# One DMA order for the loads and the weights, wider engine choice and a state without its zero blocks, in an RWKV-5 attention and squared-ReLU MLP kernel

## The chip, the cores and the metric

The kernel runs on one core of a Trainium2 chip. The metric is the device time of one launch in microseconds. The core has five engines that each work through their own queue in order: TensorE (PE in the profile, with its weight loads shown apart as PEld), VectorE (DVE), ScalarE (ACT), GpSimd (POOL) and SyncE (SP), which here only issues DMAs. Sixteen DMA engines move the data. An instruction that waits holds back everything behind it on its queue.

## What is computed

The reference is a linear-attention recurrence with decay, followed by a two-layer MLP without biases. With batch B=4, H=8 heads, S=768 steps and head width D=48:

```python
for t in range(S):
    cur = einsum('bhd,bhe->bhde', u[None] * kt, vt)
    y[:, :, t] = einsum('bhd,bhde->bhe', rt, state + cur)
    state = w[None, :, :, None] * state + einsum('bhd,bhe->bhde', kt, vt)
x = y.transpose(0, 2, 1, 3).reshape(B * S, H * D)     # 3072 x 384
h = x @ w_in                                          # 384 x 2048
r = np.maximum(h, 0.0)
return (r * r) @ w_out                                # 2048 x 384
```

Inputs and output are float32. The kernel multiplies in bfloat16 and accumulates in float32.

## The kernel before

**Units.** The sequence is cut into 6 chunks of C=128 steps. A unit is one chunk of one batch, so there are NU=24, numbered chunk by chunk over the four batches: unit n continues the state that unit n-4 left. Heads go in pairs, with each head padded from 48 to 64 rows, so a pair fills the 128 partitions.

**Attention of one unit** (lines 435 to 560). Three loads bring kt, rt and vt (192 KB each). `kw` and `rw` multiply k and r by powers of the decay and write them side by side into the buffer krp in bfloat16. ScalarE casts v to `vb`. `rk`, `rku`, `du` and `dv` make the term of the current step: r times k, times u, summed over a head, times v. krp is transposed to `rkT`: for units 0 to 9 (`NT = 10`) by TensorE and a copy, from unit 10 on by a DMA transpose that SyncE issues (line 481). `am` multiplies k with r inside the chunk, `mask` keeps the strict triangle (`AT`), `ym` multiplies AT with v and adds r times the state, and `yb` adds dv. The result is transposed to `xt`, again by TensorE or by DMA (line 573).

**State.** `kvm` makes the new product of k and v for each pair in one matmul. As two heads share a matmul, its output has a 2 by 2 grid of blocks: the two diagonal ones are the heads' own, the other two mix heads. `sma` adds the product to the old state, `smo` multiplies by the decay over the chunk `wc`, and `sbo` casts the result to bfloat16 for `ym` of unit n+4. The tiles `sm`, `sb` and `wc` are 128 x (4 pairs, 2 heads, 48), that is 384 columns, and `wc` is zero in the mixed blocks.

**MLP.** Two units make a pair (L=2, 256 rows). For each of 8 parts of the hidden layer, `m1` runs 6 matmuls (line 591), `relu` goes to VectorE or ScalarE, `sq` to ScalarE or GpSimd, and `m2` runs 2 matmuls for each unit (line 620). `osb` copies a finished unit out of PSUM and SyncE stores it.

**Weights.** w_in and w_out come in five pieces each (`PIECES`, of 1, 1, 2, 2 and 2 of the 8 parts), issued by GpSimd, which alone casts on the way.

**The order.** All of this is declared as operations with a cost per engine, a key (a due time), dependences and buffers. The function `schedule` places them one after another in a model of the engines and of the DMA, always the one that can start first; on a tie the lower key wins, with a surcharge (`away`, 8.0) for an engine that is not the operation's first. The instructions are then emitted in that order, so the order on every queue is fixed by the plan, while on the chip each waits for what it really needs. `port=True` marks products that use the port shared by VectorE and GpSimd. The plan keeps such a product on VectorE from starting before the last instruction of GpSimd ends, and GpSimd from starting inside one of VectorE. The helper `both` (line 440) gives a product GpSimd as its first engine, and VectorE as the second one for units below `NDVE`.

**The feed.** The loads of units 0 to 3 come first. Then the ten weight pieces, w_in and w_out by turns: the first two wait for the last load of unit 2, and each later one for the piece three before it. The first load of unit 4 waits for the eighth of the ten pieces. These gates are real waits; the other entries in the list of dependences of a load (the load four before it, and the last one) only guide the plan. Each of kt, rt and vt has 8 buffers (`NLOAD`).

```python
for n in range(4):
    for nm in ("kt", "rt", "vt"):
        load(n, nm)
w_ops = []
for i in range(len(PIECES) - 1):
    for which in ("in", "out"):
        w_ops.append(weights(i, which, w_ops[-3] if len(w_ops) >= 3 else units[2]["vt"]))
for n in range(4, NU):
    for nm in ("kt", "rt", "vt"):
        load(n, nm, w_ops[-3] if n == 4 and nm == "kt" else None)
```

**In the profile** most products have line 324 and most copies line 329 (ScalarE) or 331 (VectorE), the lines of the helpers, so they are told apart by their tiles: `krp<-kt,wk` is kw, `krp<-rt,wr` is rw, `sm<-bank,sm` is sma, `sm<-sm,wc` is smo, `sb<-sm` is sbo. L390 is the loads, L411 and L413 the weights, L516 am, L535 and L540 ym, L634 the stores, L310 and L313 memsets at the start.

Of the kernel before, what the change touches and what calls it, by code (L numbers as in the profile page):

```python
# [8 lines left out]
F32 = mybir.dt.float32  # L9
BF16 = mybir.dt.bfloat16  # L10
AF = mybir.ActivationFunctionType
ALU = mybir.AluOpType
# [24 lines left out]

def schedule(ops, depth, limits, free, away, warm_until=0.0, noise=None, keyf=None, bias=0.0):

    rings = {r: [] for r in depth}  # L40
# [11 lines left out]
    lastP = lastV = None  # L52
    base = {}

# [50 lines left out]
    while ready:  # L105
        best = None
        for o in ready:
            t = base.get(o)
            if t is None:
                t = 0.0  # L110
                for d, lat in o.deps:
                    t = max(t, d.end + (d.lat if lat is None else lat))
                base[o] = t
            if best is not None and t + bias * o.key > best[0][0]:
# [5 lines left out]
            if best is not None and t + bias * o.key > best[0][0]:  # L120
                continue
            chosen = ()
            if any(bf.ring in limits for bf in o.takes):
                got = pick_banks(o, t)
                if got is None:
                    continue
                t, chosen = got
            first = True
            for e in o.eng:
                s = max(t, free[e])  # L130
                if e == "V" and o.port and lastP is not None and lastP[1] > s:
                    s = lastP[1]
                elif e == "P" and lastV is not None and lastV[2] and lastV[1] > s >= lastV[0]:
                    s = lastV[1]
                rank = (s + bias * o.key, o.key + (0.0 if first else away.get(e, 0.0)), s)
# [6 lines left out]
        cost = o.eng[e]  # L142
        if noise is not None:
            cost *= noise(o)
# [36 lines left out]
def kernel(  # L181
# [11 lines left out]
    nc = tc.nc  # L193
# [19 lines left out]
    NT = 10  # L213
    NDVE = 6
    PIECES = (0, 1, 2, 4, 6, 8)
    AHEAD = 4
    LAG = 4.0
    DEPTH = 4

# [80 lines left out]
    wr = const.tile([128, H, D], F32)  # L300
    wc = const.tile([128, NP, 2, D], F32)
    ub = const.tile([128, H, D], F32)
# [6 lines left out]
    for i in range(NPADS):  # L309
        nc.vector.memset(make["krp"][i], 0.0)  # L310
    make_identity(nc, identb)
    make_upper_triangular(nc, smask, val=1.0, diag=False)
    nc.vector.memset(wc, 0.0)  # L313

# [48 lines left out]
    def emit_wcb(e):  # L363
        for i in range(2):
            rows = slice(i * PAD, i * PAD + D)
            nc.scalar.copy(wc[rows, :, i, :], wcs[rows, :, None].to_broadcast([D, NP, D]))

    o_wc = op("wc", {"A": 0.6}, 1.1, [o_wcs], emit_wcb)
    o_ub = op("ub", {"V": 0.5, "A": 0.45}, 0.5, [o_ubp],
# [14 lines left out]
    def load(n, nm, gate=None):  # L384
# [20 lines left out]
    def weights(i, which, gate):  # L405
# [3 lines left out]
        def f(e):  # L409
# [12 lines left out]

    for n in range(4):
        for nm in ("kt", "rt", "vt"):
            load(n, nm)
    w_ops = []
    for i in range(len(PIECES) - 1):
        for which in ("in", "out"):
            w_ops.append(weights(i, which, w_ops[-3] if len(w_ops) >= 3 else units[2]["vt"]))
    for n in range(4, NU):  # L430
        for nm in ("kt", "rt", "vt"):
            load(n, nm, w_ops[-3] if n == 4 and nm == "kt" else None)


    for n in range(NU):
# [42 lines left out]
        else:  # L478
# [3 lines left out]
                    out=T("rkT").rearrange("p w a c -> p (w a) c"), in_=T("krp").rearrange("p w h d -> p (w h d)")),  # L482
                takes=[X["rkT"]], uses=[X["krp"]], lat=0.05, dma=(0.7, 1.05, 0.95))
        if c < NCH - 1:
# [13 lines left out]
            old = units[n - B]["sm"] if c else None  # L498
            SM = lambda x: make[x.ring][x.slot]
            if c:  # L500
                q["sma"] = op(f"sma{n}", {"V": 0.48}, K + 3, [q["kvm"], units[n - B]["smo"]],
                              tt(lambda sm=sm: SM(sm), kvp, lambda old=old: SM(old), ALU.add), uses=[sm, kv_p, old])
                q["smo"] = op(f"smo{n}", both(0.96, 0.48), K + 5, [q["sma"]],
                              tt(lambda sm=sm: SM(sm), lambda sm=sm: SM(sm), lambda: wc, ALU.mult), uses=[sm], port=True)
            else:
                q["smo"] = op(f"smo{n}", {"V": 0.48}, K + 5, [q["kvm"], o_wc],
                              tt(lambda sm=sm: SM(sm), kvp, lambda: wc, ALU.mult), uses=[sm, kv_p])
# [55 lines left out]
    for j in range(NU // L):  # L563
# [111 lines left out]
```

## Time and profile before

| | |
|---|---|
| Time, median of 3 runs | 190.45 us (190.41 to 193.27) |
| The profiled execution | 192.72 us |
| Its span, from first to last instruction | 191.0 us |
| Mean granted TensorE clock | 0.991 |
| HBM read, written | 20.65 MB, 4.72 MB |

The profile is of a single execution. A group line reads: source line, engine, operation, output and inputs with their shapes, count; then busy time in us and mean ns of one; then the idle time of that engine just before, with what ended it. A line of the waits reads: who waited, for what, total us, how often, the longest. A line of the timeline reads: start, duration, engine, line, operation, with the idle time before it in brackets. In the table by stretch, the granted clock, the share of the DMA engines and the GB/s stand at the end of a line.

### The profile page before, as it was taken

How to read it: one execution, taken by the hardware profiler on the slowest of the kernel's cores; microseconds unless marked ns; L12 is line 12 of the kernel's file. 1: busy time of each engine (PE TensorE's matmuls, PEld its weight loads, DVE VectorE, ACT ScalarE, POOL GpSimd, SP SyncE). 2: the span in 40 equal slices, each digit the busy share in tenths (PEclk: the TensorE clock that was granted, in tenths of full speed). 3: DMA queues.
4: the chain of work that ended last, by engine and by line, in shares of the span. 5: the costliest groups of instructions: out<-in, count | busy, mean ns of one | idle time of the engine just before them, and what ended most of it. 6: DMA issues, size and time to landing. Idle time of an engine off the chain costs nothing.

```text
span 191.0 us, 4343 instructions
## 1 busy us (share of the span) xinstructions
PE 172.1 (90%) x1653; PEld 121.7 (64%) x1653; DVE 125.7 (66%) x217; ACT 109.3 (57%) x195; POOL 139.4 (73%) x158
## 2 busy tenths in 40 slices
PE   6998679798979999949998896999999999999992
PEld 2654356575757767637766675777777677777760
DVE  6265366487776668735687577689688786765741
ACT  3663347257669596624857547467665464663641
POOL 2899988499899989993888899799999994000000
PEclk9999999999999999997999999999999999999999
DMA  5999899989899999993989999435632444040202
GB/s 108 204 207 146 118 181 162 204 170 244 170 207 245 189 199 192 217 220 89 201 174 151 257 183 121 128 75 152 87 79 85 80 131 101 0 106 21 88 0 84
DMA packets 103256, 27.56 MB, mean 144 GB/s; under 512 B 96065, under 2 KB 103234, under 8 KB 103234
## 3 DMA queue, kind: packets, MB, share of 16 engines
q1 hardware_dynamic: 99088, 24.13, 61.4%
q0 software_dynamic: 4128, 3.15, 11.8%
q8 instruction: 13, 0.21, 0.5%
q14 instruction: 9, 0.07, 0.2%
q10 hardware_dynamic: 18, 0.00, 0.0%
HBM read 20.65 MB, written 4.72 MB: 133 GB/s over the span
## 4 chain that ended last, share of the span: by engine, by line
PE 52%; DMA 22%; POOL 13%; SPq 5%; issue 3%; ACT 3%; DVE 1%; DVEq 0%; POOLq 0%; ACTq 0%
PE bank L620 23%; PE bank L591 21%; DMA rkT<-krp 8%; SPq L390 5%; POOL krp L324 4%; DMA vt<-in_v_dram 4%; DMA w_in_sb<-in_moe_w_in_dram 3%; DMA w_out_sb<-in_moe_w_out_dram 3%; PE bank L516 3%; POOL rku L324 3%; POOL rk L324 2%; DMA wb<-in_w_dram 2%; DMA xt<-yb 2%; PE bank L540 2%; PE bank L535 1%
## 5 line engine op out<-in xcount | busy, mean ns | idle before, releaser
L620 PE MATMUL bank<-w_out_sb,g 128*128 128x384 bf16 x384 | 81.5, 329 | 0.9 <-ACT rkT L329 0.6
L591 PE MATMUL bank<-xt,w_in_sb 128*128 128x256 bf16 x576 | 78.9, 274 | 3.3 <-DMA w_in_sb<-in_moe_w_in_dram 2.5
L611 ACT ACTIVATE g<-gr 128x512 bf16<-128x512 f32 x93 | 57.7, 629 | 36.0 <-DVE gr L603 35.6
L603 DVE TENSOR_SCALAR gr<-bank 128x512 f32<-128x512 f32 x73 | 50.4, 691 | 31.3 <-PE bank L591 26.8
L591 PEld LDWEIGHTS <-w_in_sb 128*128 128x128 bf16 x576 | 54.6, 98 | 17.9 <-DMA w_in_sb<-in_moe_w_in_dram 3.2
L620 PEld LDWEIGHTS <-g 128*128 128x128 bf16 x384 | 34.4, 98 | 16.0 <-ACT g L611 1.2
L524 DVE TENSOR_TENSOR AT<-bank,smask 128x512 bf16<-128x512 f32 x48 | 30.8, 684 | 8.6 <-PE bank L516 8.0
L324 POOL TENSOR_TENSOR dv<-vb,du 128x384 f32<-128x384 bf16 x24 | 20.0, 832 | 11.7 <-DVE du L456 10.7
L324 POOL TENSOR_TENSOR krp<-kt,wk 128x384 bf16<-128x384 f32 x24 | 24.1, 1003 | 3.7 <-ACT wk L353 3.7
L324 POOL TENSOR_TENSOR rk<-rt,kt 128x384 f32<-128x384 f32 x24 | 24.0, 1002 | 0.4 <-DMA rt<-in_r_dram 0.3
L324 POOL TENSOR_TENSOR rku<-rk,ub 128x384 f32<-128x384 f32 x24 | 24.1, 1005 | 0.1
L324 POOL TENSOR_TENSOR krp<-rt,wr 128x384 bf16<-128x384 f32 x24 | 24.1, 1006 | 0.0
L329 ACT CAST vb<-vt 128x384 bf16<-128x384 f32 x24 | 12.2, 510 | 15.8 <-DMA vt<-in_v_dram 9.4
L548 DVE TENSOR_TENSOR yb<-bank,dv 128x384 bf16<-128x384 f32 x24 | 13.3, 555 | 11.3 <-PE bank L540 6.9
L605 ACT ACTIVATE gr<-bank 128x512 f32<-128x512 f32 x23 | 13.5, 593 | 6.3 <-PE bank L591 5.7
L324 POOL TENSOR_TENSOR sm<-sm,wc 128x384 f32<-128x384 f32 x16 | 16.0, 1000 | 1.0 <-DVE sm L324 0.9
L516 PE MATMUL bank<-rkT 48*128 48x128 bf16 x192 | 9.7, 222 | 6.8 <-DMA rkT<-krp 5.8
L516 PEld LDWEIGHTS <-rkT 48*128 48x128 bf16 x192 | 5.5, 95 | 13.7 <-DMA rkT<-krp 6.7
L456 DVE TENSOR_REDUCE du<-rku 128x8 f32<-128x384 f32 x24 | 13.1, 544 | 1.0 <-POOL rku L324 1.0
L329 ACT CAST sb<-sm 128x384 bf16<-128x384 f32 x20 | 10.1, 506 | 5.2 <-DVE sm L324 4.7
L540 PE MATMUL bank<-vb,AT 128*128 128x48 bf16 x192 | 11.7, 187 | 0.5 <-DVE AT L524 0.5
L540 PEld LDWEIGHTS <-AT 128*128 128x128 bf16 x192 | 10.3, 99 | 2.8 <-issue 0.9
(49 smaller groups left out, 127.5 us busy)
## 6 DMA issues: line engine op xcount, KB each, us to landing
kt<-in_k_dram SPq DMA_DIRECT2D x24, 192.0 KB, 3.8
rt<-in_r_dram SPq DMA_DIRECT2D x24, 192.0 KB, 3.8
vt<-in_v_dram SPq DMA_DIRECT2D x24, 192.0 KB, 3.7
out_dram<-osb SPq DMA_DIRECT2D x24, 192.0 KB, 2.2
w_in_sb<-in_moe_w_in_dram POOLq DMA_DIRECT2D x3, 384.0 KB, 6.8
w_out_sb<-in_moe_w_out_dram POOLq DMA_DIRECT2D x3, 384.0 KB, 6.9
w_in_sb<-in_moe_w_in_dram POOLq DMA_DIRECT2D x2, 192.0 KB, 4.2
w_out_sb<-in_moe_w_out_dram POOLq DMA_DIRECT2D x2, 192.0 KB, 4.2
```

The lines of the kernel that those rows point to most:

```text
L324: return lambda e: NOW[e].tensor_tensor(dst(), a(), b_(), f)
L329: nc.scalar.copy(dst(), src())
L456: lambda e, T=T: nc.vector.tensor_reduce(T("du"), T("rku"), axis=mybir.AxisListType.X, op=ALU.add),
L516: nc.tensor.matmul(out=psv(at[i], NP, C)[:, p, :], lhsT=T("rkT")[rows, 1, p, :], rhs=T("rkT")[rows, 0, p, :], start=True, stop=True,)
L524: lambda e, T=T, i=i, x=x: nc.vector.tensor_tensor(T("AT")[:, i], psv(x, NP, C), smask[:, None, :].to_broadcast([128, NP, C]), ALU.mult),
L540: nc.tensor.matmul(out=t[:, p, i, :], lhsT=T("AT")[:, i, p, :], rhs=T("vb")[:, 2 * p + i, :], start=st is None, stop=True, skip_group_chec ...
L548: lambda e, T=T, y_p=y_p: nc.vector.tensor_tensor(T("yb"), psv(y_p, HD), T("dv").rearrange("t h d -> t (h d)"), ALU.add),
L591: nc.tensor.matmul(out=psv(h, 2, L * C)[:, z], lhsT=w_in_sb[:, kk, (2 * f + z) * 128 : (2 * f + z + 1) * 128], rhs=XT()[:, kk].rearrange(" ...
L603: nc.vector.tensor_scalar(dst, src, 0.0, None, ALU.max)
L605: nc.scalar.activation(dst, src, AF.Relu)
L611: nc.scalar.activation(dst, src, AF.Square)
L620: nc.tensor.matmul(out=psv(o_p, dm), lhsT=G()[:, 2 * f + z, i, :], rhs=w_out_sb[:, 2 * f + z, :], start=(f == 0 and z == 0), stop=(f == NH ...
```

## The change

1. The feed has one order: loads of units 0 to 3, all of w_in, loads of units 4 and 5, all of w_out, loads of units 6 on. The first piece of w_in waits for the load that is fifth from the end at that point (rt of unit 2), and the first of w_out likewise (rt of unit 4). The other pieces have no gate. The first load after a group of weights waits for the last but one piece of that group.
2. `NDVE` goes from 6 to 24: VectorE is a second choice for the shared-port products of every unit.
3. `sm` and `wc` hold 192 columns, each head's own block only. `sma`, the first chunk's `smo`, and `sbo` become two instructions each, one for each half of the partitions, as they read or write blocks at different columns. The later `smo` stays one instruction, with half the columns. All `sb` buffers lie in one tile `sb_all` that is cleared once at the start; `sbo` writes the two diagonal blocks. `wc` is filled by one copy, and its memset goes.
4. The planner's model of DMAs is new: other times for loads and transposes, SyncE runs at most three DMAs ahead, a stall of 1 us every 12.4 us, and other start times of the engines. Arguments that were not used (noise, keyf, bias) go.

```diff
-def schedule(ops, depth, limits, free, away, warm_until=0.0, noise=None, keyf=None, bias=0.0):
+def schedule(ops, depth, limits, free, away, stalls, warm_until=0.0):
...
             x0 = max(s + pre, free["D"])
-            free["D"] = x0 + xf
-            o.xs, o.end = x0, x0 + xf + post
-            free[e] = s + cost if e == "P" else max(s + cost, x0 - 0.2)
+            x1 = x0 + xf + sum(d for at, d in stalls if x0 <= at < x0 + xf)
+            free["D"], o.end = x1, x1 + post
+            free[e] = s + cost
+            if e == "S":
+                queue.append(x1)
+                if len(queue) > 2:
+                    free[e] = max(free[e], queue[-3])
...
-    NDVE = 6
+    NDVE = 24
...
+    BEFORE, BEHIND = 5, 1
+    FEED = (("units", 0, 4), ("in", 0, 5), ("units", 4, 6), ("out", 0, 5), ("units", 6, NU))
...
+    sb_all = const.tile([128, 2 * B, NP, 2, D], BF16)
     for b in range(B):
-        sb_ring(f"sm{b}", 2, [128, NP, 2, D], F32)
-        sb_ring(f"sb{b}", 2, [128, NP, 2, D], BF16)
+        sb_ring(f"sm{b}", 2, [128, NP, D], F32)
+        depth[f"sb{b}"], make[f"sb{b}"] = 2, [sb_all[:, 2 * b + i] for i in range(2)]
...
+    nc.vector.memset(sb_all, 0.0)
     make_identity(nc, identb)
     make_upper_triangular(nc, smask, val=1.0, diag=False)
-    nc.vector.memset(wc, 0.0)
...
-        for i in range(2):
-            rows = slice(i * PAD, i * PAD + D)
-            nc.scalar.copy(wc[rows, :, i, :], wcs[rows, :, None].to_broadcast([D, NP, D]))
+        nc.scalar.copy(wc, wcs[:, :, None].to_broadcast([128, NP, D]))
...
-        if len(loads) >= DEPTH:
-            deps.append((loads[-DEPTH], 0.0))
         if loads:
-            deps.append((loads[-1], -9.0))
-        q[nm] = op(f"{nm}{n}", {"S": 0.55}, PACE * (n - AHEAD), deps, f, takes=[q["_" + nm]], lat=0.05, dma=(0.65, 0.9, 1.75))
+            deps.append((loads[-1], -40.0))
+        q[nm] = op(f"{nm}{n}", {"S": 0.55}, PACE * (n - AHEAD), deps, f, takes=[q["_" + nm]], lat=0.05, dma=(0.65, 0.95, 1.8))
...
-        o = op(f"w_{which}{i}", {"P": 0.77}, -5 + 0.1 * i, [(gate, 0.05)] if gate is not None else [], f, lat=0.05,
+        o = op(f"w_{which}{i}", {"P": 0.77}, -5 + 0.1 * i, [(gate, 0.05)] if gate is not None else [(w_ops[-1], -40.0)], f, lat=0.05,
...
+    w_ops, after = [], None
+    for what, lo, hi in FEED:
+        if what == "units":
+            for n in range(lo, hi):
+                for nm in ("kt", "rt", "vt"):
+                    load(n, nm, after)
+                    after = None
+        else:
+            for i in range(lo, hi):
+                gate = loads[-BEFORE] if i == lo else None
+                w_ops.append(weights(i, what, gate))
+            after = w_ops[-1 - BEHIND]
...
-                takes=[X["rkT"]], uses=[X["krp"]], lat=0.05, dma=(0.7, 1.05, 0.95))
+                takes=[X["rkT"]], uses=[X["krp"]], lat=0.05, dma=(0.7, 1.2, 1.1))
...
+            def halves(f):
+                def g(e):
+                    for i in range(2):
+                        f(e, slice(i * PAD, (i + 1) * PAD), i)
+                return g
             if c:
-                q["sma"] = op(f"sma{n}", {"V": 0.48}, K + 3, [q["kvm"], units[n - B]["smo"]],
-                              tt(lambda sm=sm: SM(sm), kvp, lambda old=old: SM(old), ALU.add), uses=[sm, kv_p, old])
-                q["smo"] = op(f"smo{n}", both(0.96, 0.48), K + 5, [q["sma"]],
+                q["sma"] = op(f"sma{n}", {"V": 0.56}, K + 3, [q["kvm"], units[n - B]["smo"]],
+                              halves(lambda e, rows, i, kvp=kvp, sm=sm, old=old: nc.vector.tensor_tensor(
+                                  SM(sm)[rows], kvp()[rows, :, i, :], SM(old)[rows], ALU.add)), uses=[sm, kv_p, old])
+                q["smo"] = op(f"smo{n}", both(0.5, 0.28), K + 5, [q["sma"]],
...
-            q["sbo"] = op(f"sbo{n}", {"A": 0.41}, K + 6, [q["smo"]],
-                          copy(lambda sb=sb: SM(sb), lambda sm=sm: SM(sm)), takes=[sb], uses=[sm])
+            q["sbo"] = op(f"sbo{n}", {"A": 0.6}, K + 6, [q["smo"]],
+                          halves(lambda e, rows, i, sb=sb, sm=sm: nc.scalar.copy(SM(sb)[rows, :, i, :], SM(sm)[rows])),
+                          takes=[sb], uses=[sm])
...
-                    takes=[xt] if i == 0 else [], uses=[q["_yb"]] + ([xt] if i else []), lat=0.05, dma=(0.9, 0.4, 1.0)))
+                    takes=[xt] if i == 0 else [], uses=[q["_yb"]] + ([xt] if i else []), lat=0.05, dma=(0.9, 0.6, 1.1)))
...
-        free={"T": 4.0, "V": 3.6, "A": 4.0, "P": 2.3, "D": 2.4, "S": 1.2, "W": 3.2},
+        free={"T": 4.0, "V": 4.2, "A": 4.4, "P": 2.3, "D": 2.7, "S": 1.2, "W": 3.2},
+        stalls=[(18.3 + 12.4 * i, 1.0) for i in range(16)],
         away={"V": 8.0, "A": 8.0, "P": 8.0}, warm_until=WARM_UNTIL)
```

More of the change, by code (lines that the diff above doesn't have):

```diff
@@ L52, in schedule @@
     lastP = lastV = None
-    base = {}
+    base, queue = {}, []
     def ring_time(o):
@@ L113, in schedule @@
                 base[o] = t
-            if best is not None and t + bias * o.key > best[0][0]:
+            if best is not None and t > best[0][0]:
                 continue
@@ L119, in schedule @@
             t = max(t, r)
-            if best is not None and t + bias * o.key > best[0][0]:
+            if best is not None and t > best[0][0]:
                 continue
@@ L134, in schedule @@
                     s = lastV[1]
-                rank = (s + bias * o.key, o.key + (0.0 if first else away.get(e, 0.0)), s)
+                rank = (s, o.key + (0.0 if first else away.get(e, 0.0)), s)
                 first = False
@@ L142, in schedule @@
         cost = o.eng[e]
-        if noise is not None:
-            cost *= noise(o)
         o.start, o.by = s, e
@@ L300 @@
     wr = const.tile([128, H, D], F32)
-    wc = const.tile([128, NP, 2, D], F32)
+    wc = const.tile([128, NP, D], F32)
     ub = const.tile([128, H, D], F32)
@@ L363, in emit_wcb @@
     def emit_wcb(e):
[L364 to L368 removed]
+        nc.scalar.copy(wc, wcs[:, :, None].to_broadcast([128, NP, D]))
+    o_wc = op("wc", {"A": 0.35}, 1.1, [o_wcs], emit_wcb)
     o_ub = op("ub", {"V": 0.5, "A": 0.45}, 0.5, [o_ubp],
@@ L421, in weights @@
         return o
[L423 to L432, printed above, removed]
+    w_ops, after = [], None
[10 more added lines that the diff above has]
+            after = w_ops[-1 - BEHIND]
     for n in range(NU):
@@ L499 @@
             SM = lambda x: make[x.ring][x.slot]
+            def halves(f):
[3 more added lines that the diff above has]
+                return g
             if c:
-                q["sma"] = op(f"sma{n}", {"V": 0.48}, K + 3, [q["kvm"], units[n - B]["smo"]],
-                              tt(lambda sm=sm: SM(sm), kvp, lambda old=old: SM(old), ALU.add), uses=[sm, kv_p, old])
-                q["smo"] = op(f"smo{n}", both(0.96, 0.48), K + 5, [q["sma"]],
+                q["sma"] = op(f"sma{n}", {"V": 0.56}, K + 3, [q["kvm"], units[n - B]["smo"]],
+                              halves(lambda e, rows, i, kvp=kvp, sm=sm, old=old: nc.vector.tensor_tensor(
+                                  SM(sm)[rows], kvp()[rows, :, i, :], SM(old)[rows], ALU.add)), uses=[sm, kv_p, old])
+                q["smo"] = op(f"smo{n}", both(0.5, 0.28), K + 5, [q["sma"]],
                               tt(lambda sm=sm: SM(sm), lambda sm=sm: SM(sm), lambda: wc, ALU.mult), uses=[sm], port=True)
             else:
-                q["smo"] = op(f"smo{n}", {"V": 0.48}, K + 5, [q["kvm"], o_wc],
-                              tt(lambda sm=sm: SM(sm), kvp, lambda: wc, ALU.mult), uses=[sm, kv_p])
-            q["sbo"] = op(f"sbo{n}", {"A": 0.41}, K + 6, [q["smo"]],
-                          copy(lambda sb=sb: SM(sb), lambda sm=sm: SM(sm)), takes=[sb], uses=[sm])
+                q["smo"] = op(f"smo{n}", {"V": 0.56}, K + 5, [q["kvm"], o_wc],
+                              halves(lambda e, rows, i, kvp=kvp, sm=sm: nc.vector.tensor_tensor(
+                                  SM(sm)[rows], kvp()[rows, :, i, :], wc[rows], ALU.mult)), uses=[sm, kv_p])
+            q["sbo"] = op(f"sbo{n}", {"A": 0.6}, K + 6, [q["smo"]],
+                          halves(lambda e, rows, i, sb=sb, sm=sm: nc.scalar.copy(SM(sb)[rows, :, i, :], SM(sm)[rows])),
+                          takes=[sb], uses=[sm])
         at = [Buf("a"), Buf("a")]
```

1 line of the change is left out of this document (removed).

## The prediction, written before the changed kernel ran

> **What bounds the kernel now.** I read the page first: its first two parts and the shares of the chain.
>
> ```profile
> span 191.0 us, 4343 instructions
> PE 172.1 (90%) x1653; PEld 121.7 (64%) x1653; DVE 125.7 (66%) x217; ACT 109.3 (57%) x195; POOL 139.4 (73%) x158
> DMA  5999899989899999993989999435632444040202
> PE 52%; DMA 22%; POOL 13%; SPq 5%; issue 3%; ACT 3%; DVE 1%; DVEq 0%; POOLq 0%; ACTq 0%
> ```
>
> TensorE is busy 90% of the span and over half of the chain, so the end is TensorE's work plus the time it stands still. The DMA engines are full for the first 23 or so of the 40 slices (about 110 us). To see where TensorE stands still I cut the span where its waits change and read the busy table by stretch (columns: stretch, length, then busy time and instructions of PE, PEld, DVE, ACT, POOL, then granted clock, DMA share, GB/s).
>
> ```profile
> 21.40:31.40 10.00, 8.30 (x85) 6.15 (x84) 5.09 (x9) 5.53 (x9) 9.03 (x11) 1.00 1.16 169
> 31.40:37.40 6.00, 5.00 (x50) 2.98 (x49) 4.36 (x8) 2.79 (x6) 2.76 (x4) 1.00 1.11 185
> 37.40:80.70 43.30, 41.01 (x447) 30.35 (x445) 31.51 (x55) 30.60 (x57) 41.08 (x44) 1.00 0.97 203
> 80.70:120.00 39.30, 33.33 (x330) 24.03 (x330) 25.93 (x45) 22.09 (x40) 32.72 (x36) 0.96 0.96 177
> 120.00:180.00 60.00, 60.00 (x592) 44.49 (x591) 44.52 (x75) 35.27 (x61) 37.40 (x41) 1.00 0.36 85
> 180.00:191.00 11.00, 7.20 (x51) 4.62 (x49) 3.66 (x6) 3.64 (x7) 0.00 (x0) 1.00 0.13 47
> ```
>
> Length less PE busy is the idle time: 1.70, 1.00, 2.29, 5.97, 0.00 and 3.80 us. After 120 us TensorE never stops until the drain at the end, so every microsecond that it loses earlier arrives at the end, and every one given back leaves it. There are 10.96 us to be had between 21.4 and 120. The waits, the timelines of TensorE and SyncE, and the clock say what they are.
>
> ```profile
> PE bank L516 <- DMA rkT<-krp: 5.8, 3, 2.9
> PE bank L591 <- DMA w_in_sb<-in_moe_w_in_dram: 2.5, 2, 1.6
> 83.64 0.40 PE L516 MATMUL bank<-rkT 48*128 48x128 bf16 x8 [2.93 <-DMA rkT<-krp]
> 79.00 0.91 SPq L390 DMA_DIRECT2D vt<-in_v_dram  x1
> 80.03 1.54 SPq L481 DMA_TRANSPOSE rkT<-krp  x1
> 80.00:90.00 10.00, 7.07 (x59) 4.90 (x56) 4.76 (x8) 4.09 (x8) 7.37 (x8) 0.83 0.83 164
> 86.00:87.00 1.00, 1.00 (x14) 0.79 (x13) 0.38 (x1) 0.00 (x0) 1.00 (x2) 0.50 1.02 211
> ```
>
> The largest single loss is the 2.93 us before 83.64. Loads stood ahead of the transpose on SyncE's queue (the last issued at 79.00, the transpose at 80.03), and the matmuls had been written into TensorE's order for an earlier arrival. Soon after it the granted clock falls to 0.50, and over these ten microseconds its mean is 0.83: another 10 x 0.17 = 1.7 us lost. The planner wrote an order for a faster DMA than the chip gave it.
>
> **The change, part by part.** *The feed.* Today the weight pieces alternate and each waits for the third before it, while SyncE holds unit 4's loads back.
>
> ```profile
> SPq L390 <- DMA w_out_sb<-in_moe_w_out_dram: 18.3, 1, 18.3
> 10.00:12.00 2.00, 2.00 (x19) 1.22 (x18) 0.95 (x3) 1.27 (x3) 2.00 (x3) 1.00 1.04 204
> 18.00:20.00 2.00, 1.73 (x12) 0.64 (x9) 0.56 (x1) 0.51 (x1) 1.53 (x3) 1.00 0.89 106
> 26.00:28.00 2.00, 2.00 (x27) 1.57 (x28) 1.97 (x4) 0.63 (x1) 1.72 (x3) 1.00 1.27 206
> 13.18 0.93 POOL L411 DMA_DIRECT2D w_in_sb<-in_moe_w_in_dram  x1
> 18.73 0.76 POOL L411 DMA_DIRECT2D w_in_sb<-in_moe_w_in_dram  x1 [0.45 <-DMA w_out_sb<-in_moe_w_out_dram]
> 21.90 0.81 PE L591 MATMUL bank<-xt,w_in_sb 128*128 128x256 bf16 x6
> 31.30 0.37 SPq L390 DMA_DIRECT2D kt<-in_k_dram  x1
> 38.09 1.00 POOL L324 TENSOR_TENSOR krp<-kt,wk 128x384 bf16<-128x384 f32 x1
> 41.84 1.12 SPq L634 DMA_DIRECT2D out_dram<-osb  x2
> 47.58 0.66 PE bank L591 x6
> rt<-in_r_dram SPq DMA_DIRECT2D x24, 192.0 KB, 3.8
> w_out_sb<-in_moe_w_out_dram POOLq DMA_DIRECT2D x2, 192.0 KB, 4.2
> ```
>
> (The last two rows give the median from issue to landing; the one before them is a step of the chain, one m1.) The ten weight issues stay ten on GpSimd, at about 0.8 us each; none is added. Five of them lie between 13.18 and 19.5 now, and the five w_in issues will; the 0.45 us wait goes and no piece comes between the products, so the first m1 (21.90) starts about 0.4 us earlier, between 0 and 1. With the large pieces in flight, and no loads beside them, the engines move 206 GB/s, with small pieces and the throttle 106. Unthrottled I take 200 for w_in: 8 units of 196,608 bytes are 1.57 MB, 7.9 us, from about 15 (12 loads and wb at 0.95 us each, 196,608 bytes at the 204 to 207 of these rows, begun at about 2.5 us) to 23. w_in3 ends 2 of the 8 units before that and lands at about 22, so kt4, gated on it, goes out then instead of at 31.30. GpSimd can begin unit 4 after ten issues and twelve products of units 1 to 3, 13.18+8+12 = 33.2, instead of 38.09. Behind kt4's wait on SyncE stands nothing that is due: the first store goes out at 41.84. The first w_out waits on GpSimd for rt4, 22+3.8, about 26, with products of unit 3 behind it that are not urgent before 33, and lands 4.2 later at about 30. Until then TensorE holds m1 of pair 0 (8 at 0.66, 5.3 us) and some 2.4 us of attention for units 2 and 3 (31 small matmuls each, under the 0.05 us of the eight at 83.64): work to 21.5+7.7 = 29.2. So the waits of 2.5 us for w_in go and about 1 us for w_out comes, with another microsecond while m2 follows the pieces. Idle 21.4 to 37.4: 2.70 becomes 1.9, between 1.0 (w_out never late) and 6 (below).
>
> *37 to 80 us.* GpSimd is busy 41.08 of 43.30 here and gets a lead of four to five microseconds from unit 4's earlier data. I let half of the 2.29 us go: minus 1.2, between 0 and minus 2.3.
>
> *The state.* Three sets of instructions change, with these rows of the groups by shape:
>
> ```profile
> L324 POOL TENSOR_TENSOR sm<-sm,wc 128x384 f32<-128x384 f32 x16 | 16.0, 1000 | 1.0 <-DVE sm L324 0.9
> L613 POOL TENSOR_TENSOR g<-gr 128x512 bf16<-128x512 f32 x3 | 3.1, 1039 | 2.6 <-DVE gr L603 2.1 <-DMA vt<-in_v_dram 0.4
> L324 DVE TENSOR_TENSOR sm<-bank,sm 128x384 f32<-128x384 f32 x16 | 8.9, 554 | 1.9 <-PE bank L491 1.4
> L524 DVE TENSOR_TENSOR AT<-bank,smask 128x512 bf16<-128x512 f32 x48 | 30.8, 684 | 8.6 <-PE bank L516 8.0 <-ACT g L611 0.5
> L329 ACT CAST sb<-sm 128x384 bf16<-128x384 f32 x20 | 10.1, 506 | 5.2 <-DVE sm L324 4.7 <-POOL sm L324 0.4
> L366 ACT COPY wc<-wcs 48x192 f32<-48x192 f32 x2 | 0.7, 348 | 0.0
> L310 DVE MEMSET krp<- 128x512 uint32 x4 | 1.9, 485 | 0.2
> L313 DVE MEMSET wc<- 128x384 f32 x1 | 0.4, 378 | 0.0
> L331 DVE COPY ub<-bank 128x384 f32<-128x384 f32 x1 | 0.6, 558 | 1.2 <-PE bank L345 1.2
> L324 POOL TENSOR_TENSOR krp<-kt,wk 128x384 bf16<-128x384 f32 x24 | 24.1, 1003 | 3.7 <-ACT wk L353 3.7
> ```
>
> GpSimd's smo halves its elements: half of 1000 ns if time goes by size, 0.94 us if by the slope from 384 to 512 elements (39 ns over 128); the 512 row multiplies a tensor by itself, so I stay near half, 0.58, saving 16 x 0.42 = 6.7 us of GpSimd (between 1 and 8). The Trainium skill (GPSIMD Engine Reference, Elementwise — side-by-side cycle accounting) gives about 2.6 cycles per element for two inputs, at 1.2 GHz; an estimate from it for 192 elements fewer is 0.42 us, against 0.06 by the slope between the rows; no run here shows a 192-element product yet. VectorE: (684-554)/128 = 1.02 ns per element, so a half takes 554-195 = 359 and two 718: 0.16 us more, 20 times, 3.3 us in all. ScalarE: two copies at 348 for one at 506: 0.19 us more, 20 times, 3.8 us. Neither engine bounds a stretch (31.51 and 30.60 busy of 43.30), and the state is used four units later; what stands in line behind them (relu, square) can slip a little: plus 0.4, between 0 and 2. sb_all's memset (1536 words, by the slope from 378 to 485 about 1.34 us) takes the place of 0.38 in front of the copy of ub, which stood idle 1.2 us for TensorE: nothing, at most 0.2. One wc copy in place of two saves ScalarE 0.35 us that no later row waits for: nothing too, like the unused arguments that leave the planner.
>
> *VectorE for products of every unit.* Units 0 to 5 could do so already, yet all 24 krp products ran on GpSimd. In the planner a shared-port product on VectorE starts no sooner than GpSimd's last instruction ends, and GpSimd is listed first and without the surcharge of 8. It can never win. Nothing: the widening is empty.
>
> *The new times for DMA.* Loads 0.95, transposes 1.2 and 0.6, three in SyncE's queue, and a stall of 1 us every 12.4. Between 80.7 and 120 the idle 5.97 us come mostly from transposes behind loads. With later arrivals planned, matmuls that were ready are put ahead: I let 3.5 go, between plus 1 and minus 5; this is the least certain term. With a gap under 2.9 us the dip of the clock goes too, minus 1.7; if the gap stays, nothing.
>
> Sum against the profiled execution (192.72 us, of which 191.0 is the span): -0.4 -0.8 -1.2 -3.5 -1.7 +0.4 = -7.2, so **185.5 us**. That execution is 2.27 us above the median of 190.45, about what the clock's dip and a longer wait cost; against the median the gain is 4.95 us, 2.6%. Some 2% is what can be told from no change here: 186.6 and 194.3 are the bounds.
>
> **Rivals.** *The gaps only move.* For it: 206 GB/s is one stretch, and the transposes still share full engines with the loads; their waits come back under other names. Against: the first stop of DMA throttling is plain in the 106 row. Then only the start and the clock are gained: 192.72-0.4-0.8-1.7 = 189.8, chance 0.27.
>
> *w_out comes too late: slower.* w_in at the 106 GB/s of the early row takes 1.57/0.106 = 14.8 us and lands at 29 to 30; kt4 goes at 28, rt4 lands at 32, w_out0 at 36. GpSimd, which issues in order, waits at w_out0 with the products of unit 3 behind it, and TensorE is out of work from 29.2: a gap of 6.8 us, followed by 1.7 us at half clock as after the 2.93 us gap; less the 2.70 us lost there today that is +5.8, so 190.45+5.8 = 196.3 with no gain elsewhere. It decides from a w_out0 later than about 34. Chance 0.1. The Trainium skill (TensorE: Matmul & The Clock Gate, Part 1: The HAM clock gate) says that the clock falls to half after an idle window of about 3.4 us, and needs as long a busy one to recover; by it a gap of 1 us here costs itself alone. The trace differs a little: 2.93 us were enough, and the measurement decides.
>
> *VectorE does take products.* Then each moves 1.0 us from GpSimd to about 0.55 on VectorE, with GpSimd halted meanwhile: net 0.45 us a product. That could take what GpSimd still costs between 37 and 80, 2.29-1.2 = 1.1 us: 184.4, but the 24 of 24 row speaks against it; chance 0.03.
>
> *All gaps close.* 192.72-10.96-1.7-0.4 = 179.7, the floor; nearly that, 181, chance 0.06.
>
> **The numbers.** The forecast has 0.54, the others 0.27, 0.1, 0.03 and 0.06. Of the forecast's own spread (182.5 to 188) a tenth lies above 186.6, so faster is 0.9 x 0.54+0.03+0.06 = 0.58, same 0.05+0.27 = 0.32, slower 0.10. The range runs from 181.3 to 191.5: it takes in the moved gaps and leaves out the late w_out and the floor.
>
> **What would show it.** Right: w_in issues five in a row near 13 us; kt4 near 22; unit 4's first product on GpSimd near 33; no wait of TensorE for w_in over 0.5 us and one of about 1 us for w_out near 29; sm on GpSimd near 0.58 us; no product on VectorE; waits for rkT under 3 us together and the clock at 1.00 throughout. Wrong: kt4 after 27, a dip of the clock near 32, or rkT waits of 5 us again.

## The result, and the profile after

The changed kernel takes 184.38 us (median of 4 runs, 184.03 to 185.82); the kernel before took 191.14 us in the same comparison (190.41 to 193.27). The ratio is 0.9643, with a 95% interval of 0.9545 to 0.9741. The profiled execution took 184.36 us, with a span of 182.5. The profiled execution of the kernel before, 192.72 us, was a slow one of its kind, so the two profiles lie 8.4 us apart and the medians 6.8. Line numbers have moved by a few lines: m1 is L601 (was L591), m2 L630 (L620), am L526 (L516), the loads L391 (L390), w_in L410 and w_out L412.

The page of the changed kernel, its first part and the shares of the chain:

```profile
span 182.5 us, 4374 instructions
PE 169.4 (93%) x1656; PEld 121.2 (66%) x1656; DVE 130.7 (72%) x236; ACT 113.1 (62%) x216; POOL 131.0 (72%) x157
PE 79%; DMA 7%; POOL 6%; DVE 4%; issue 1%; ACT 1%; DVEq 0%; POOLq 0%
```

TensorE's share of the chain went from 52% to 79% and that of the DMA from 22% to 7%: the end is now set by TensorE's own work. VectorE and ScalarE have gained 5.0 and 3.8 us of work and GpSimd has lost 8.4. The table by stretch, with the same bounds up to 120 us:

```profile
21.40:31.40 10.00, 7.72 (x92) 6.26 (x90) 8.65 (x16) 6.95 (x13) 10.00 (x13) 1.00 1.13 200
31.40:37.40 6.00, 4.79 (x46) 3.46 (x47) 3.87 (x8) 3.38 (x9) 6.00 (x8) 1.00 1.23 174
37.40:80.70 43.30, 42.42 (x469) 31.59 (x468) 32.86 (x62) 33.71 (x66) 41.55 (x48) 1.00 1.00 203
80.70:120.00 39.30, 38.52 (x393) 28.32 (x392) 32.13 (x59) 25.42 (x51) 37.85 (x45) 1.00 0.92 186
```

TensorE's idle time is 2.28, 1.21, 0.88 and 0.78 us: 5.15 in place of 10.96. By stretch that is +0.58, +0.21, -1.41 and -5.19 us. With the 1.7 us of the clock's dip between 80 and 90 us, which is gone, 7.5 of the 8.5 us between the two spans are placed; the last microsecond isn't. Most of it, 6.9 us, comes from behind 80 us, and the beginning has become worse. Three of TensorE's waits:

```profile
PE bank L630 <- DMA w_out_sb<-in_moe_w_out_dram: 2.4, 3, 1.3
PE bank L471 <- POOL krp L327: 1.9, 3, 0.9
PE bank L601 <- DMA xt<-yb: 0.8, 1, 0.8
```

The waits for rkT (5.8 us) and for w_in (2.5 us) are not in the list any more. In place of the second there is a wait for w_out of nearly the same size. The timeline of the beginning, from GpSimd, SyncE and TensorE (cut at the dots):

```profile
12.68 4.01 POOL L410 DMA_DIRECT2D w_in_sb<-in_moe_w_in_dram  x5
16.72 1.01 POOL L327 TENSOR_TENSOR rk<-rt,kt 128x384 f32<-128x384 f32 x1
17.67 1.00 POOL L327 TENSOR_TENSOR krp<-kt,wk 128x384 bf16<-128x384 f32 x1
18.62 0.99 POOL L327 TENSOR_TENSOR rku<-rk,ub 128x384 f32<-128x384 f32 x1
19.58 0.99 POOL L327 TENSOR_TENSOR krp<-rt,wr 128x384 bf16<-128x384 f32 x1
20.54 0.98 POOL L327 TENSOR_TENSOR rk<-rt,kt 128x384 f32<-128x384 f32 x1
21.49 0.82 POOL L327 TENSOR_TENSOR dv<-vb,du 128x384 f32<-128x384 bf16 x1
...
27.83 3.73 POOL L412 DMA_DIRECT2D w_out_sb<-in_moe_w_out_dram  x5
...
32.33 1.04 POOL L327 TENSOR_TENSOR krp<-kt,wk 128x384 bf16<-128x384 f32 x1
```

```profile
23.53 0.37 SPq L391 DMA_DIRECT2D kt<-in_k_dram  x1
```

```profile
23.87 0.81 PE L601 MATMUL bank<-xt,w_in_sb 128*128 128x256 bf16 x6 [0.57 <-ACT xt L332]
31.92 0.82 PE L630 MATMUL bank<-w_out_sb,g 128*128 128x384 bf16 x4 [1.34 <-DMA w_out_sb<-in_moe_w_out_dram]
```

The feed runs as the diff says: five w_in issues in a row, kt4 at 23.53 instead of 31.30, unit 4 on GpSimd at 32.33 instead of 38.09. But the first m1 starts at 23.87, two microseconds later than before. dv of unit 1, which pair 0 needs, starts at 21.49 instead of 19.50. Five weight issues stood ahead of it in the kernel before too. What is new are the two products of unit 2 at 19.58 and 20.54 (rw and rk, 0.96 us from start to start), which stood behind it in the kernel before:

```profile
19.50 0.84 POOL L324 TENSOR_TENSOR dv<-vb,du 128x384 f32<-128x384 bf16 x1
...
21.11 1.01 POOL L324 TENSOR_TENSOR krp<-rt,wr 128x384 bf16<-128x384 f32 x1
...
22.87 1.01 POOL L324 TENSOR_TENSOR rk<-rt,kt 128x384 f32<-128x384 f32 x1
```

The groups by shape that the compact state changed:

```profile
L327 POOL TENSOR_TENSOR sm<-sm,wc 128x192 f32<-128x192 f32 x16 | 9.6, 601 | 0.3 <-DVE sm L509 0.3
L509 DVE TENSOR_TENSOR sm<-bank,sm 64x192 f32<-64x192 f32 x32 | 11.3, 354 | 4.8 <-PE bank L491 4.3
L518 ACT CAST sb_all<-sm 64x192 bf16<-64x192 f32 x40 | 13.8, 345 | 5.7 <-DVE sm L515 4.1 <-POOL sm L327 1.1
L314 DVE MEMSET sb_all<- 128x1536 uint32 x1 | 1.3, 1338 | 0.3 <-issue 0.3
L327 POOL TENSOR_TENSOR krp<-kt,wk 128x384 bf16<-128x384 f32 x24 | 24.2, 1009 | 5.6 <-ACT wk L356 3.8
```

A half of sma takes 354 ns, a half of sbo 345, and smo on GpSimd 601 in place of 1000. All 24 kw products are still on GpSimd.

### The profile page after: what moved, and what is told of

Its sections match the earlier page's. It is cut to its first block, busy times and chain, and to the rows that moved or that the text cites. A ratio compares the mean times of both kernels' runs of the same rounds, so it can differ in the third digit from the quotient of the medians.

```text
span 182.5 us, 4374 instructions
## 1 busy us (share of the span) xinstructions
PE 169.4 (93%) x1656; PEld 121.2 (66%) x1656; DVE 130.7 (72%) x236; ACT 113.1 (62%) x216; POOL 131.0 (72%) x157
## 4 chain that ended last, share of the span: by engine, by line
PE 79%; DMA 7%; POOL 6%; DVE 4%; issue 1%; ACT 1%; DVEq 0%; POOLq 0%
PE bank L630 32%; PE bank L601 31%; DMA w_out_sb<-in_moe_w_out_dram 5%; PE bank L526 3%; POOL w_in_sb L410 2%; PE bank L550 2%; PE bank L545 2%; PE bank L320 2%; DVE gr L613 2%; DMA xt<-yb 2%; PE bank L491 2%; POOL krp L327 2%; PE bank L471 2%; POOL dv L327 1%; PE bank L342 1%
## 5 line engine op out<-in xcount | busy, mean ns | idle before, releaser
L630 PE MATMUL bank<-w_out_sb,g 128*128 128x384 bf16 x384 | 80.6, 326 | 2.6 <-DMA w_out_sb<-in_moe_w_out_dram 2.4
L621 ACT ACTIVATE g<-gr 128x512 bf16<-128x512 f32 x94 | 58.3, 629 | 35.3 <-DVE gr L613 34.4
L601 PE MATMUL bank<-xt,w_in_sb 128*128 128x256 bf16 x576 | 77.6, 272 | 1.3 <-DMA xt<-yb 0.8
L613 DVE TENSOR_SCALAR gr<-bank 128x512 f32<-128x512 f32 x75 | 51.2, 689 | 21.1 <-PE bank L601 18.3
L601 PEld LDWEIGHTS <-w_in_sb 128*128 128x128 bf16 x576 | 54.9, 98 | 14.3 <-issue 1.6
L630 PEld LDWEIGHTS <-g 128*128 128x128 bf16 x384 | 34.2, 97 | 17.8 <-DMA w_out_sb<-in_moe_w_out_dram 1.5
L518 ACT CAST sb_all<-sm 64x192 bf16<-64x192 f32 x40 | 13.8, 345 | 5.7 <-DVE sm L515 4.1
L509 DVE TENSOR_TENSOR sm<-bank,sm 64x192 f32<-64x192 f32 x32 | 11.3, 354 | 4.8 <-PE bank L491 4.3
L615 ACT ACTIVATE gr<-bank 128x512 f32<-128x512 f32 x21 | 12.4, 593 | 2.7 <-PE bank L601 2.3
L320 PE MATMUL bank<-zb 128*128 128x512 bf16 x32 | 11.0, 462 | 1.7 <-DVE zb L308 1.7
L550 PEld LDWEIGHTS <-AT 128*128 128x128 bf16 x192 | 9.8, 96 | 2.7 <-issue 1.2
L332 ACT COPY osb<-bank 128x384 f32<-128x384 f32 x14 | 6.6, 476 | 6.0 <-PE bank L630 6.0
```

The source lines that it names most:

```text
L320: nc.tensor.matmul(out=banks[7], lhsT=zb[:, :128], rhs=zb, start=True, stop=True, skip_group_check=True)
L332: nc.scalar.copy(dst(), src())
L518: halves(lambda e, rows, i, sb=sb, sm=sm: nc.scalar.copy(SM(sb)[rows, :, i, :], SM(sm)[rows])),
L550: nc.tensor.matmul(out=t[:, p, i, :], lhsT=T("AT")[:, i, p, :], rhs=T("vb")[:, 2 * p + i, :], start=st is None, stop=True, skip_group_chec ...
L601: nc.tensor.matmul(out=psv(h, 2, L * C)[:, z], lhsT=w_in_sb[:, kk, (2 * f + z) * 128 : (2 * f + z + 1) * 128], rhs=XT()[:, kk].rearrange(" ...
L613: nc.vector.tensor_scalar(dst, src, 0.0, None, ALU.max)
```

## The experiments

The change has three parts that can be put in one by one: the feed (F), the compact state (S) and the planner's new DMA model (P: times, stalls, SyncE's queue, start times). The wider engine choice is a fourth only in name: with `NDVE = 6` and with 24 the changed kernel has the same instructions in the same order on every engine, so it has no run of its own. Each ratio below is to the kernel before on the same chip. Four kernels ran first, on one chip, each with some parts in.

```diff
# F alone: feed as in the change; the state and the planner's model as before
+    FEED = (("units", 0, 4), ("in", 0, 5), ("units", 4, 6), ("out", 0, 5), ("units", 6, NU))
...
+                gate = loads[-BEFORE] if i == lo else None
+                w_ops.append(weights(i, what, gate))
```

> The kernel before with the new feed alone (old state, old planner times). Theory A (the terms of the prediction add): about 2 us off, 188.5, from the waits for w_in and GpSimd's earlier unit 4; the waits for rkT (5.8 us) stay. Rival B (the smaller state does it, by GpSimd's relief): no change, 190.5. Rival C (the parts only work together, since the gaps move): within 1 us of before or slower.

Measured: 189.28 us, ratio 0.9813 (0.9738 to 0.9887). The time is near theory A's, and its reasons hold in part. Unit 4 is earlier on GpSimd (31.73), and TensorE's idle time from 37.4 to 80.7 us falls from 2.29 to 0.59. But from 21.4 to 37.4 it grows from 2.70 to 3.34, and the waits for rkT do not stay: from 80.7 to 120 us the idle time is 4.07 against 5.97, with these two waits:

```profile
PE bank L591 <- DMA xt<-yb: 2.5, 1, 2.5
PE bank L516 <- DMA rkT<-krp: 1.7, 2, 1.6
```

```diff
# S alone
-        sb_ring(f"sm{b}", 2, [128, NP, 2, D], F32)
+        sb_ring(f"sm{b}", 2, [128, NP, D], F32)
...
+            q["sbo"] = op(f"sbo{n}", {"A": 0.6}, K + 6, [q["smo"]],
+                          halves(lambda e, rows, i, sb=sb, sm=sm: nc.scalar.copy(SM(sb)[rows, :, i, :], SM(sm)[rows])),
```

> The kernel before with the compact state alone. Theory A: GpSimd's smo at 601 ns takes 6.4 us off GpSimd, but GpSimd is not what ends TensorE's long waits, so 190 to 191, with the waits for rkT still above 4 us. Rival B: 186 or less, the waits for rkT under 3 us. Rival C: within 1 us of before.

Measured: 193.35 us, ratio 1.0079 (1.0041 to 1.0117): slower, if by less than 1%. The 190 to 191 of theory A are missed, and its waits for rkT are not there; one for xt is (below).

```diff
# P alone
+            x1 = x0 + xf + sum(d for at, d in stalls if x0 <= at < x0 + xf)
...
+        stalls=[(18.3 + 12.4 * i, 1.0) for i in range(16)],
...
-                takes=[X["rkT"]], uses=[X["krp"]], lat=0.05, dma=(0.7, 1.05, 0.95))
+                takes=[X["rkT"]], uses=[X["krp"]], lat=0.05, dma=(0.7, 1.2, 1.1))
```

> The kernel before with the planner's new DMA model alone. Theory A: the largest single part, 3.5 to 5 us off, 186 to 187, waits for rkT under 3 us in all, clock at 1.00 between 80 and 120. Rival B: 190. Rival C: within 1 us of before.

Measured: 186.74 us, ratio 0.9700 (0.9616 to 0.9785). All that theory A said holds: TensorE waits 0.9 us for rkT, its idle time from 80.7 to 120 us is 2.65 us, and the clock there is at 1.00.

```diff
# F and P: the changed kernel with the old state
-        sb_ring(f"sm{b}", 2, [128, NP, D], F32)
+        sb_ring(f"sm{b}", 2, [128, NP, 2, D], F32)
...
```

> The changed kernel with the old state (feed and planner new). Theory A: the state is worth under 1 us, so 184 to 185.5. Rival B: 188 or more. Rival C: between 186 and 190, as the state's shorter GpSimd work is needed for the rest to count.

Measured: 183.68 us, ratio 0.9521 (0.9446 to 0.9596), a little below theory A. Then the two other pairs, on another chip:

```diff
# F and S: the changed kernel with the old planner's model
-            x1 = x0 + xf + sum(d for at, d in stalls if x0 <= at < x0 + xf)
-            free["D"], o.end = x1, x1 + post
+            free["D"] = x0 + xf
+            o.xs, o.end = x0, x0 + xf + post
...
```

> The changed kernel with the old DMA model in the planner (feed and state new). Theory A: 188 to 189, the waits for rkT back at 4 to 6 us. Rival B: 185. Rival C: 187 to 191, in no way the sum of the two parts run alone.

Measured: 192.02 us, ratio 1.0032 (0.9991 to 1.0073). Theory A's 188 to 189 are missed, and again it is xt that is waited for, not rkT.

```diff
# S and P: the changed kernel with the old feed
-    for what, lo, hi in FEED:
+    for i in range(len(PIECES) - 1):
+        for which in ("in", "out"):
+            w_ops.append(weights(i, which, w_ops[-3] if len(w_ops) >= 3 else units[2]["vt"]))
...
```

> The changed kernel with the old feed (state and planner new). Theory A: 186 to 187, the waits for w_in back at about 2.5 us and unit 4 on GpSimd near 38 us again. Rival B: 185 or less. Rival C: 187 to 191.

Measured: 184.25 us, ratio 0.9677 (0.9637 to 0.9717). Theory A's time is missed, and rival B's is met; w_in is waited for again (1.6 us), and unit 4 starts on GpSimd at 38.29.

What follows: P is the part that matters. It takes 3.0% alone, 2.9% on top of F (0.9813 to 0.9521), 4.0% on top of S (1.0079 to 0.9677) and 3.9% on top of both (1.0032 to 0.9643). F takes 1.9% alone and 1.8% beside P, but with S in the kernel nearly nothing: 0.5% and 0.3%, inside the intervals. Ratios from two chips are to be taken with care: F and P gave 0.9521 on the first and 0.9603 on the second (below), at 183.68 and 183.32 us. Rival B, that the smaller state does it, falls: F and P without S are as fast as the whole, and neither S alone nor F and S are faster than before. What S is worth beside P alone stays open: 184.25 us with it and 186.74 without, but on two chips, and 0.9677 against 0.9700 as ratios. Rival C, that the parts only work together, falls for P and F. S and F do not add up without P: alone they would multiply to 0.9890, and together they gave 1.0032. The two kernels with S and the old model show where the time went, in TensorE's waits of S alone and of F and S:

```profile
PE bank L597 <- DMA xt<-yb: 5.2, 1, 5.2
```

```profile
PE bank L599 <- DMA xt<-yb: 5.8, 1, 5.8
```

Each has one long stop of TensorE for a DMA transpose, where the kernel before had three for rkT, and between 80.7 and 120 us the granted clock is 0.91 in both, against 0.96 in the kernel before and with F alone. With the new model the wait for xt is 0.8 us in the changed kernel. Why the old plan stops at that place with S and not without it is not known.

Three kernels on one chip asked what the compact state costs once F and P are in.

```diff
# F and P again, with the old state
# the changed kernel again: no edit
# the compact state, planned with the costs of the old one
...
-                q["sma"] = op(f"sma{n}", {"V": 0.56}, K + 3, [q["kvm"], units[n - B]["smo"]],
+                q["sma"] = op(f"sma{n}", {"V": 0.48}, K + 3, [q["kvm"], units[n - B]["smo"]],
...
-                q["smo"] = op(f"smo{n}", both(0.5, 0.28), K + 5, [q["sma"]],
+                q["smo"] = op(f"smo{n}", both(0.96, 0.48), K + 5, [q["sma"]],
...
-            q["sbo"] = op(f"sbo{n}", {"A": 0.6}, K + 6, [q["smo"]],
+            q["sbo"] = op(f"sbo{n}", {"A": 0.41}, K + 6, [q["smo"]],
```

> The changed kernel with the old state once more, beside the two below on one chip. If the compact state costs time, this is about 1 us faster than the changed kernel; if the first comparison was only the chip's, the two are within 0.3 us.

Measured: 183.32 us, ratio 0.9603 (0.9553 to 0.9654).

> The changed kernel itself, on the same chip. Theory D (the state costs by its longer VectorE and ScalarE work): about 1 us behind the old state. Theory E (the state costs only because it makes the planner draw another order): the same 1 us behind, but see the next run. Theory A of the prediction: at most 0.4 us behind.

Measured: 184.35 us, ratio 0.9620 (0.9571 to 0.9668).

> The changed kernel with the planner's costs of the old state for sma, smo, sbo and wc: the compact state's instructions stand in exactly the order that the old state's have. Theory D: slower than the old state by 1 us, like the changed kernel. Theory E: equal to the old state within 0.3 us, or up to 0.5 us faster, since GpSimd's smo is 0.4 us shorter.

Measured: 183.41 us, ratio 0.9605 (0.9547 to 0.9664).

The state's instructions in the old state's order take 183.41 against 183.32 us, so theory D, a cost of the instructions themselves of 1 us, is not borne out. The changed kernel's median is 1 us above both, which is what theory E says and more than the 0.4 of theory A. But the three intervals are about 1 us wide to each side and lie on one another, so none of the three is excluded, and whether the plan that belongs to the compact state is worse stays open. A version that is faster than the changed kernel is not shown.

The last three kernels took the planner's model apart, on a third chip, all with the new feed and the old state. The new start times of VectorE and ScalarE are in all three and were not taken apart. The first also has the old times for xt and the old start of the DMA.

```diff
# old times
-        q[nm] = op(f"{nm}{n}", {"S": 0.55}, PACE * (n - AHEAD), deps, f, takes=[q["_" + nm]], lat=0.05, dma=(0.65, 0.95, 1.8))
+        q[nm] = op(f"{nm}{n}", {"S": 0.55}, PACE * (n - AHEAD), deps, f, takes=[q["_" + nm]], lat=0.05, dma=(0.65, 0.9, 1.75))
...
-                takes=[X["rkT"]], uses=[X["krp"]], lat=0.05, dma=(0.7, 1.2, 1.1))
+                takes=[X["rkT"]], uses=[X["krp"]], lat=0.05, dma=(0.7, 1.05, 0.95))
```

> New feed, old state, new queue model and stalls, but the old planned times of loads (0.9, was 0.95), of both transposes (1.05 and 0.4, were 1.2 and 0.6) and the old start of the DMA. If the times carry the planner's gain: 187 or more, with transposes waited for again (over 3 us). If the queue model or the stalls do: within 1 us of the new one, 184 to 185.

Measured: 186.96 us, ratio 0.9669 (0.9604 to 0.9733).

```diff
# old queue
-            free[e] = s + cost
-            if e == "S":
-                queue.append(x1)
-                if len(queue) > 2:
-                    free[e] = max(free[e], queue[-3])
+            free[e] = s + cost if e == "P" else max(s + cost, x0 - 0.2)
...
+        if len(loads) >= 4:
+            deps.append((loads[-4], 0.0))
```

> New feed, old state, new times and stalls, but SyncE as it was planned before: held until its last DMA starts, and a load planned only after the load four before it has landed. If the queue model carries the gain: 187 or more. If not: 184 to 185.

Measured: 183.62 us, ratio 0.9497 (0.9435 to 0.9559).

```diff
# no stalls
-        stalls=[(18.3 + 12.4 * i, 1.0) for i in range(16)],
+        stalls=[],
```

> New feed, old state, new times and queue model, without the stall of 1 us every 12.4 us. It is 8% of the planned DMA time, more than the 5% on a load, so by theory A (the plan ran ahead of the chip's DMA) it should cost 1 to 3 us: 185 to 187. If the plan was right without it: 184 to 185.

Measured: 187.93 us, ratio 0.9728 (0.9659 to 0.9797).

On that chip the kernel with the old queue model is as fast as any, so for this part of the model no gain in time shows. Beside it, the old times cost 1.8% (0.9669 over 0.9497) and leaving out the stalls 2.4%, the latter a little more than expected. The table of the stretch from 80.7 to 120 us, first without stalls, then with the old times, then with the old queue, then with the whole model (F and P again, on the second chip):

```profile
80.70:120.00 39.30, 35.56 (x369) 25.89 (x366) 28.21 (x48) 21.93 (x40) 34.91 (x38) 1.00 1.00 175
```

```profile
80.70:120.00 39.30, 37.55 (x387) 27.45 (x385) 30.07 (x52) 21.85 (x41) 36.79 (x40) 1.00 0.88 189
```

```profile
80.70:120.00 39.30, 37.90 (x388) 27.46 (x386) 30.34 (x52) 23.62 (x43) 37.98 (x41) 1.00 1.04 190
```

```profile
80.70:120.00 39.30, 39.30 (x410) 29.17 (x411) 32.09 (x55) 23.57 (x45) 38.68 (x42) 1.00 0.92 190
```

TensorE's idle time there is 3.74, 1.75, 1.40 and 0.00 us, against 5.97 in the kernel before. In that stretch both transposes are waited for again without the stalls, and xt alone with the old times and with the old queue, in this order:

```profile
PE bank L593 <- DMA xt<-yb: 2.2, 2, 1.3
PE bank L518 <- DMA rkT<-krp: 1.6, 1, 1.6
```

```profile
PE bank L593 <- DMA xt<-yb: 1.8, 2, 1.3
```

```profile
PE bank L591 <- DMA xt<-yb: 1.4, 2, 1.0
```

So the stretch carries the loss of the kernel without stalls: 2.34 us of idle time more than with the old queue, where the profiled spans are 1.6 us apart. It does not carry that of the old times, whose 1.8 us of waits are short of the 3 expected and only 0.4 more than with the old queue. Over the whole span the old times have no more idle time than the old queue (13.4 and 13.7 us), but a lower granted clock (0.976 and 0.996). How much of their 1.8% is the transposes' stays open.

Whether a plan ran ahead of the chip can be read directly: the planner gives each load a planned landing, and the trace has the real one. For kt of unit 0 the two are within 0.4 us in every kernel of this table, and for kt of unit 17, which the kernel before issues at 77.42, ahead of its long stop, they are (us):

| Kernel | planned | landed | late |
|---|---|---|---|
| before | 72.24 | 80.97 | 8.73 |
| F alone | 69.82 | 77.15 | 7.33 |
| S alone | 73.43 | 83.26 | 9.83 |
| F and S | 73.06 | 79.60 | 6.54 |
| P alone | 79.89 | 82.82 | 2.93 |
| S and P | 81.09 | 83.79 | 2.70 |
| F and P again | 80.50 | 82.53 | 2.03 |
| the changed kernel | 81.70 | 84.27 | 2.57 |
| the same, its second profile | 81.70 | 81.59 | -0.11 |
| F and P without stalls | 73.10 | 76.78 | 3.68 |
| F and P with the old times | 78.28 | 81.78 | 3.50 |
| F and P with the old queue | 80.50 | 82.88 | 2.38 |

With the old model kt comes 6.5 to 9.8 us late, with the new one at most 2.9, and 3.5 to 3.7 with the stalls or the times taken back. In the kernel before the arrears grow on the way: 3.09 us for kt of unit 4, 4.57 for unit 8, 6.95 for unit 13. The load itself lands no earlier in the changed kernel than in the kernel before; the plan has it later.

## Why the prediction was right, and where it was not

The forecast of 185.5 us stands against 184.38; its sum of -7.2 us from the profiled execution against -8.4 (192.72 to 184.36). Against the median of 190.45 it was -4.95, and the medians moved by 6.8. The mechanism that it called the largest is the one that works, but that the total came out so near is partly luck: the beginning was wrong by about 2 us, and the stretch behind 80.7 made up for it.

*The planner's model (-3.5): right.* Idle time between 80.7 and 120 us fell by 5.19 us in all. By one profile each, P alone takes 3.32 away (5.97 to 2.65), near the forecast, and F alone 1.90, which the forecast did not have: it let the feed work only up to 80 us.

*The clock (-1.7): as forecast between these two profiles, but in part luck.* Between 80 and 90 us it is back at 1.00:

```profile
80.00:90.00 10.00, 10.00 (x108) 7.73 (x107) 7.92 (x15) 6.99 (x14) 10.00 (x12) 1.00 0.85 187
```

That the dip goes with a gap of 2.93 us is not the whole rule: the clock of the changed kernel fell to 0.50 in another execution without such a gap (last section). Over all executions listed with the runs, the mean granted clock is 0.9858 for the kernel before (44) and 0.9905 for the changed kernel (10). An estimate from that is just under 1 us (0.0047 of 190), and not 1.7.

*The reason given,* that the plan ran ahead of the chip's DMA, is shown by the table of planned and real landings, and by leaving out the planned stalls, which brings the waits for both transposes back. The old times cost time too, but their one profile leaves open by which wait. The forecast named the four changes together; for the third, SyncE's queue, no gain shows.

*The start (-0.4): wrong.* The prediction counted the same five issues ahead of the first m1 and took only a wait away. It did not ask which products the planner would put behind the issues. The first m1 came 1.97 us later, since dv of unit 1 slipped from 19.50 to 21.49, behind two products of unit 2. Part of it shows as idle time, part as warm-up matmuls (32 in place of 29).

*21 to 37 us (-0.8): wrong in sign, +0.79.* The waits for w_in went and those for w_out came, as said, and of their 2.4 us only 1.54 lie in this stretch. The step that failed is the start again: 1.46 us of idle time lie between 21.4 and the first m1 at 23.87, and 0.48 more in a wait for krp at 33.42, and the forecast had neither. The marks on the way were near: kt4 at 23.53 (22), w_out from 27.83 (26), unit 4 on GpSimd at 32.33 (33.2). GpSimd did not wait at rt4's gate (the product before starts at 26.88 and takes 1.00 us, the issues begin at 27.83), and the slower rival did not come about.

*37 to 80 us (-1.2): -1.41, but the reason is not shown.* GpSimd's lead is there; yet P alone, with unit 4 on GpSimd at 37.90, takes 1.21 us away here too (2.29 to 1.08).

*The state (+0.4): instruction times right, the cost within what can't be told.* Predicted 580, 359 and 348 ns and a memset of 1340; measured 601, 354, 345 and 1338. The medians are 0.7 and 1.0 us higher with it, in two comparisons. The estimate for smo worked out from the Trainium skill (GPSIMD Engine Reference, Elementwise — side-by-side cycle accounting), 0.42 us less for 192 elements fewer, is near the measured 0.40. The slope between the two rows of the profile (0.06) was the wrong guide; that the 512-element row multiplies a tensor by itself may be the reason, but no run here tests it.

*The wider engine choice (nothing): right,* and not only in time: the program doesn't change, and all shared-port products stay on GpSimd.

*The rival of moved gaps* held in one place only, w_in's wait for w_out's, but S and F with the old model are such a case: the gap moves to xt and the time stays.

## What to carry to other kernels

Where an order is written ahead by a planner, an error in its DMA times adds up over the transfers (here from 3.09 to 8.73 us between two loads of kt), and is paid by the engine whose order was written for data that isn't there yet; so compare planned and real arrival times late in the run, not at the start. An option for an engine does nothing if the planner's rules never choose it: look at where the operations ran before. When DMA issues are moved on an engine that also computes, follow the products behind them to the first thing that waits for them.

## What the runs showed of the hardware

There are two profiles of the changed kernel, with the same order of instructions. TensorE's waits between 12 and 24 us agree within 0.02 us; the clock does not. First the profile shown above, then the second one, from 20 to 26 us:

```profile
20.00:22.00 2.00, 1.20 (x8) 0.44 (x7) 0.69 (x2) 1.43 (x3) 2.00 (x3) 1.00 1.24 206
22.00:24.00 2.00, 0.87 (x13) 0.57 (x14) 1.66 (x3) 0.55 (x2) 2.00 (x3) 1.00 1.18 194
24.00:26.00 2.00, 2.00 (x26) 1.81 (x25) 1.67 (x4) 0.48 (x1) 2.00 (x4) 1.00 0.92 173
```

```profile
20.00:22.00 2.00, 1.14 (x8) 0.43 (x7) 0.63 (x2) 1.43 (x3) 2.00 (x3) 1.00 1.24 206
22.00:24.00 2.00, 0.94 (x13) 0.59 (x14) 1.73 (x4) 0.48 (x2) 2.00 (x3) 0.87 1.16 190
24.00:26.00 2.00, 2.00 (x18) 1.51 (x17) 1.14 (x3) 0.00 (x0) 2.00 (x4) 0.50 0.89 170
```

The clock fell to 0.50 in one execution and stayed at 1.00 in the other, after TensorE had been busy for 2.1 of the 4 us from 20 to 24 in both. Between 12 and 24 us it had no listed gap longer than 0.94 us in either. The Trainium skill (TensorE: Matmul & The Clock Gate, Part 1: The HAM clock gate) says that the window which the gate watches runs freely, so that the number of slow matmuls differs between runs of one kernel. These two executions agree with that. It also speaks of an idle window of about 3.4 us; here the clock fell without one, in a stretch that was about half busy. The execution with the dip was not the slower one (183.1 us against 184.36): its list has no wait for w_out, which took 2.4 us in the other, so at least part of the time of its slow matmuls would have been waited away.
